# Routed attention and a gated long convolution in one kernel: first head pair routed by head, scores per head for four pairs, some exponential sums on GpSimd, a new order of the work

## The chip, the cores and the metric

The kernel runs on one core of one Trainium2 chip. The metric is the device time of one execution in microseconds (us). Its engines are TensorE (PE; its weight loads are listed as PEld), VectorE (DVE), ScalarE (ACT), GpSimd (POOL) and the DMA queue of SyncE (SP). DMAs are issued from SP, POOL and ACT. Everything is written by hand: which engine does an operation and in which order stands in a table in the program.

## The reference

```python
# attention: q, k, v are 4 batches x 8 heads x 768 x 64; centroids 8 heads x 16 x 64
q_assign = argmax(q_n . c_n);  k_assign = argmax(k_n . c_n)     # nearest of 16 centroids
mask = q_assign[..., :, None] == k_assign[..., None, :]
scores = where(mask, q k^T / 8, -1e9)
attn = exp(scores - max);  attn = attn / (sum(attn) + 1e-9);  attn_out = attn v
# long convolution, x = attn_out as 4 x 768 x 512
x1, x2, x3 = split(x @ w_proj, 3)
y = x1 * irfft(rfft(x2) * rfft(filter)) * x3
out = y @ w_out                                                 # 4 x 768 x 512, float32
```

## The kernel before

**The unit of work is a pair of heads**: 16 pairs (4 batches of 4). `prepare(n)` makes the operands of pair n: the raw rows of q and k come in by DMA and are turned so that the 64 features lie on partitions (DVE transposes, L134; for pair 0 alone PE transposes, L125, which ACT copies out of PSUM). `routing(n)` multiplies with the normalised centroids (`SIM`, psR<-qT,cbd), and DVE finds the nearest one in four steps: transpose R1 (L158), maximum R2 (L162), compare R3 (L166), transpose back R7 (L171). A product with a constant (`TB`, psR<-ohT,tb) turns the one-hot rows into mask rows. Together with -q and k (casts `C`, L141 to L145) they make the tile `aug`, so that one product gives score and mask penalty at once. For pair 0 the mask rows go straight from PSUM into `aug` (`W`, ACT L190 or DVE L192, eight pieces); for the others by ACT or DVE into `ohS` (`R8`) and by four DMAs into `aug`.

**Then six key tiles sk per pair**: `scores` (PE, psB or psBS<-aug), the exponential (`E`, ACT), `values` (`PV`, psO<-P,v: 128 keys against 768 query columns of two heads) and `sums` (`A`, DVE L271, 128x1536 float32: acc += P, five in a row per pair, each needing the one before). Four `P` tiles rotate: one comes free when its `PV` and its `A` have run. Pairs 0 to 3 use psB: three banks of 512 columns, so a tile's two heads of 768 come as three pieces with an `E` each (L256). From pair 4 on there is one psBS tile of three banks and one `E` of 1536 columns (L233). `finish` multiplies acc with ones (`D`, psR<-acc,ones) for the denominators; in pairs 0 and 1 the last key tile is not added by DVE but multiplied with ones by PE (`DS`, psR<-P,ones, table `PES`). The reciprocals go through DMAs, and DVE makes xT (`X`).

**After each four pairs a batch is convolved**: sums and differences of halves (`XB`), the projection (`U`), the spectrum (`F`), products with the filter's spectrum (`M`, DVE L368; `Y`, DVE or POOL L375, L381), the inverse (`I`), gates (`G`, `GE`, `GM`), their product (`Y2`, DVE or POOL L436) and the output product (`O`), copied to `ob` (three tiles in rotation) and written by a DMA of SP (L458). The batch's work lies between the score and value products of the next four pairs; after the last pair only convolution is left.

**The order** is one compressed table, `ORDER`: it names every operation of the program in turn with its engine. Each engine runs its own operations in that order, and tiles are handed out and come free in it too. An operation of POOL that is listed in `PORT` (two SBUF inputs or a cast) also waits for the last such operation of DVE before it in the table. `NWU` products of zeros (`WU`, psR<-ob) fill PE's waits at the start: 36 operations of two products each. PSUM has eight banks: at first three for small things (`R`), two for `O` and three for `B`.

Of the kernel before, what the change touches and what calls it, by code (L numbers as in the profile page):

```python
# [28 lines left out]
FRONT = 1  # L29
NWU = 36  # L30
NF = 4
PES = [1, 1] + [0] * 14
DIRECT = 1
# [12 lines left out]
PCLASSES = dict(S=(1, [128, 2 * S], F32), B=(3, [128, 512], F32), O=(1, [128, 2, 512], F32), R=(8, [128, 512], F32))  # L46
# [11 lines left out]
def adder(nc, eng):  # L58
    return {"DVE": nc.vector.tensor_tensor, "POOL": nc.gpsimd.tensor_tensor}[eng]

# [16 lines left out]
def program(io):  # L77
# [15 lines left out]
    def load_front(n, j):  # L93
        b, r = divmod(n, 4)
        for hp in range(2):
            def f(hp=hp):
                nc.sync.dma_start(P["raw", n, j][:].rearrange("p (t e d) -> p t e d", t=NT, e=2)[:, :, hp],
                                  (q, k)[j][b, 2 * r + hp].rearrange("(p t) d -> p t d", t=NT))
            op(("LF", n, j, hp), "SP", f, [], [(("raw", n, j), hp)])
# [19 lines left out]
    def front_turn(n, j):  # L119
        where = lambda ch: ("BR"[j], "t", n, j, ch)  # L120
        half = lambda ch: P[where(ch)][:, :HS]
        for ch in range(2):
            def f(ch=ch):
                for t in range(3):
                    nc.tensor.transpose(half(ch)[:, ts(t, 128)], P["raw", n, j][:, ts(3 * ch + t, 128)], C["ident"])  # L125
            op(("FT", n, j, ch), "PE", f, [("raw", n, j), "ident"], [where(ch)])
        for ch in range(2):
            def f(eng, ch=ch):
                copier(nc, eng)(P["qT", n, j][:, ts(ch, HS)], half(ch))
            op(("FE", n, j, ch), ("ACT", "DVE"), f, [where(ch)], [(("qT", n, j), ch)])  # L130
# [6 lines left out]
    def cast(n, j, hp):  # L137
        def f(eng):
            o, i = P["aug", n][64 * hp:64 * hp + 64, hp, j], P["qT", n, j][64 * hp:64 * hp + 64]
# [6 lines left out]
        op(("C", n, j, hp), ("ACT", "DVE", "POOL") if j else ("ACT", "DVE"), f, [("qT", n, j)], [(("aug", n), ("x", j, hp))])  # L146

    def routing(n):
# [6 lines left out]
        op(("SIM", n), "PE", f, [("qT", n, 0), ("qT", n, 1), "cbd"], [("R", "sim", n)])  # L155

        def f():
            nc.vector.transpose(P["sT", n][:], P["R", "sim", n][:, :HS])  # L158
        op(("R1", n), "DVE", f, [("R", "sim", n)], [("sT", n)])

        def f():
            nc.vector.tensor_reduce(P["mx", n], P["sT", n][:].rearrange("p (n c) -> p n c", c=NC), axis=AX, op=Alu.max)  # L162
        op(("R2", n), "DVE", f, [("sT", n)], [("mx", n)])

        def f():
            nc.vector.tensor_tensor(P["cand", n], P["sT", n][:].rearrange("p (n c) -> p n c", c=NC),  # L166
                                    P["mx", n][:].unsqueeze(2).to_broadcast([128, 24, NC]), op=Alu.is_equal)
        op(("R3", n), "DVE", f, [("sT", n), ("mx", n)], [("cand", n)])

        def f():  # L170
            nc.vector.transpose(P["ohT", n][:], P["cand", n][:].rearrange("p n c -> p (n c)"))  # L171
        op(("R7", n), "DVE", f, [("cand", n)], [("ohT", n)])
# [5 lines left out]

        if n < DIRECT:
            for j in range(2):  # L180
                for hp in range(2):
                    for ch in range(2):
                        def f(eng, j=j, hp=hp, ch=ch):
                            z = 2 * ch + j
                            r = 32 * (2 - hp)
                            rows = slice(32 * z, 32 * z + 32)
                            o, i = P["aug", n][r:r + 32, hp, j, ts(ch, HS)], P["R", "tb", n][rows, :HS]
                            m = C["mk"][rows, hp if j else 2:hp + 1 if j else 3]
                            if eng == "ACT":
                                nc.scalar.activation(o, i, Act.Relu, **(dict(scale=m) if j else dict(bias=m)))  # L190
                            else:
                                nc.vector.tensor_scalar(o, i, m, 0.0, op0=Alu.mult if j else Alu.add, op1=Alu.max)  # L192
                        op(("W", n, j, hp, ch), ("DVE", "ACT"), f, [("R", "tb", n), "mk"], [(("aug", n), ("o", j, hp, ch))])
            return
# [22 lines left out]
    def scores(n, sk):  # L217
# [19 lines left out]
        for b, some in enumerate((parts[:1], parts[1:3], parts[3:])):  # L237
            def f(b=b, some=some):
                products(some, lambda h, c, w: P["B", n, sk, b][64 * h:64 * h + 64, ds(c - 512 * b, w)])
            need = []  # L240
            for hp, lo, hi in some:
                need += [(("aug", n), ("x", j, hp)) for j in range(2)]
                halves = {(1, sk // 3)} | {(0, x // HS) for x in (lo, hi - 1)}
                need += [(("aug", n), ("o", j, hp, ch) if n < DIRECT else ("o", j, hp)) for j, ch in sorted(halves)]
# [487 lines left out]
def routed_attention_and_long_convolution(ctx: ExitStack, tc: tile.TileContext, q, k, v, c, wp, ff, wo, out):  # L732
# [14 lines left out]
    C = {}  # L747
# [58 lines left out]
    for name in ("RO", "R", "RS"):  # L806
        banks[name].close()
# [73 lines left out]
```

## Time and profile before

| | |
|---|---|
| time, 3 runs | 366.17 us median (365.65 to 366.39) |
| the profiled execution | 365.99 us, its span 364.3 us |
| PE busy | 355.0 us, 97% |
| DVE busy | 333.6 us, 92% |
| ACT busy | 254.8 us, 70% |
| POOL busy | 90.5 us, 25% |
| first score product, first value product | at 16.13 us, at 21.77 us |
| last product ends, last write is issued | at 360.02 us, at 361.14 us |

How to read it: span times count from the first instruction, and the execution's own time is 1.7 us longer than its span. In a row of groups stand line, engine, operation, tiles (out<-in), shape and count, then busy time in us and mean ns of one, then idle time of the engine ahead of it. In a row of the timeline stand start, length, engine and what; "x20" are merged instructions. All products but transposes have line 84, so they are told apart by their tiles. A logical float32 product shows as two records.

### The profile page before, as it was taken

To read this page: it belongs to the slowest core of one execution; us is meant where nothing else is said; L and a number is where in the kernel's file an instruction comes from. 1 tells how busy PE (TensorE), PEld (TensorE's weight loads), DVE (VectorE), ACT (ScalarE), POOL (GpSimd) and SP (SyncE) were. 2 spreads that over 40 slices of the span, in tenths; PEclk is the share of its full clock that TensorE was granted. 3 is DMA by queue.
4 is the path that set the end of the run, shared out by engine and by line. 5 is a ranking of instruction groups with operands and counts; after the bars stand their busy time and mean duration, and the time that the engine had idled before them with its cause. 6 is when DMAs were issued, how large, how long until landed. Compare 5 with 4: busy or idle time off the path is not lost.

```text
span 364.3 us, 8367 instructions
## 1 busy us (share of the span) xinstructions
PE 355.0 (97%) x3273; PEld 191.2 (52%) x3273; DVE 333.6 (92%) x458; ACT 254.8 (70%) x353; POOL 90.5 (25%) x126
## 2 busy tenths in 40 slices
PE   8899999999999999999999999999999999999995
PEld 3344445454355565545445656554445555555673
DVE  7899999999989999999888999998998999975992
ACT  6899888897786877786755768778776667214332
POOL 5333300023245314230112430211000211160651
PEclk9999999999999999999999999999999999999999
DMA  8676966588794455536344236255202310112204
GB/s 164 109 128 130 226 146 124 106 151 129 144 137 90 110 111 107 118 87 168 80 82 114 56 55 134 51 139 144 75 13 68 120 45 2 46 47 88 87 2 173
DMA packets 116167, 37.37 MB, mean 103 GB/s; under 512 B 104353, under 2 KB 109793, under 8 KB 116129
## 3 DMA queue, kind: packets, MB, share of 16 engines
q1 hardware_dynamic: 112688, 31.31, 39.7%
q0 software_dynamic: 3296, 5.51, 7.3%
q8 instruction: 25, 0.41, 0.5%
q14 instruction: 14, 0.11, 0.1%
q10 hardware_dynamic: 144, 0.03, 0.0%
HBM read 30.97 MB, written 6.39 MB: 103 GB/s over the span
## 4 chain that ended last, share of the span: by engine, by line
PE 71%; DVE 18%; issue 4%; ACT 3%; DMA 2%; SPq 1%; POOL 0%; DVEq 0%; ACTq 0%
PE psO L84 27%; PE psR L84 25%; PE psBS L84 10%; DVE acc L271 8%; PE psSR L84 4%; DVE tm L368 4%; PE psB L84 3%; ACT P L233 2%; PE psOR L84 1%; DVE qT L134 1%; DVE y L381 1%; DMA raw<-in_q_dram 1%; DMA aug<-ohS 1%; SPq L109 1%; DMA out_dram<-ob 0%
## 5 line engine op out<-in xcount | busy, mean ns | idle before, releaser
L84 PE MATMUL psO<-P,v 128*64 128x512 f32 (+1 forms) x768 | 139.4, 487 | 0.2 <-ACT P L233 0.2
L233 ACT ACTIVATE P<-psBS 128x1536 f32<-128x1536 f32 x72 | 104.6, 1452 | 42.2 <-PE psBS L84 36.8
L271 DVE TENSOR_TENSOR acc<-acc,P 128x1536 f32<-128x1536 f32 x62 | 108.4, 1749 | 3.1 <-ACT P L233 1.0
L84 PEld LDWEIGHTS psO<-P,v 128*64 128x64 f32 x768 | 54.5, 136 | 66.9 <-issue 56.3
L84 PEld LDWEIGHTS <-aug 96*64 96x64 bf16 (+1 forms) x768 | 44.9, 110 | 33.4 <-issue 12.5
L84 PE MATMUL psBS<-aug 96*64 96x512 bf16 (+3 forms) x576 | 59.9, 327 | 0.3 <-ACT P L233 0.2
L256 ACT ACTIVATE P<-psB 128x512 f32<-128x512 f32 x72 | 38.1, 598 | 4.8 <-PE psB L84 4.6
L84 PE MATMUL psR<-xT,wpj 128*64 128x384 bf16 x416 | 40.8, 326 | 0.1
L84 PEld LDWEIGHTS <-wpj 128*64 128x64 bf16 x512 | 30.3, 110 | 13.5 <-issue 1.8
L375 POOL TENSOR_TENSOR y<-tm,tm 128x512 bf16<-128x512 f32 x13 | 16.4, 1273 | 63.5 <-DVE tm L368 52.2
L84 PEld LDWEIGHTS <-y 128*64 128x64 bf16 x440 | 24.9, 110 | 13.1 <-DVE y L436 0.6
L134 DVE STREAM_TRANSPOSE qT<-raw 128x768 f32<-128x768 f32 x30 | 28.8, 964 | 0.2
L436 POOL TENSOR_TENSOR y<-yy,g 128x768 bf16<-128x768 f32 (+1 forms) x14 | 20.5, 1474 | 32.2 <-DVE g L403 13.1
L330 POOL TENSOR_TENSOR xb<-xT 128x384 bf16<-128x384 bf16 x12 | 11.2, 931 | 68.0 <-DVE acc L271 27.1
L271 DVE TENSOR_TENSOR acc<-P,P 128x1536 f32<-128x1536 f32 x16 | 27.8, 1737 | 0.1
L141 POOL CAST aug<-qT 64x768 bf16<-64x768 f32 x13 | 10.7, 819 | 68.9 <-DVE acc L271 56.0
L368 DVE TENSOR_TENSOR tm<-psR,hm 128x512 f32<-128x512 f32 x40 | 25.2, 681 | 1.7 <-PE psR L84 1.3
L84 PE MATMUL psB<-aug 128*64 128x256 bf16 (+3 forms) x192 | 22.3, 328 | 0.9 <-DVE aug L192 0.6
L143 ACT ACTIVATE aug<-qT 64x768 bf16<-64x768 f32 x25 | 21.0, 841 | 1.6 <-PE psBS L84 1.1
L84 PE MATMUL psR<-uv,fw 128*64 128x512 bf16 x156 | 20.2, 379 | 0.1
L398 ACT COPY g<-psR 128x384 f32<-128x384 f32 x25 | 11.5, 483 | 12.0 <-PE psR L84 11.8
L84 PE MATMUL psR<-wpj,xb 128*64 128x512 bf16 x160 | 19.2, 379 | 0.0
(160 smaller groups left out, 439.0 us busy)
## 6 DMA issues: line engine op xcount, KB each, us to landing
rb<-dr SPq DMA_DIRECT2D x32, 192.0 KB, 3.4
out_dram<-ob SPq DMA_DIRECT2D x23, 256.0 KB, 2.2
raw<-in_q_dram SPq DMA_DIRECT2D x60, 96.0 KB, 3.1
raw<-in_k_dram SPq DMA_DIRECT2D x60, 96.0 KB, 3.4
v<-in_v_dram POOLq DMA_DIRECT2D x8, 384.0 KB, 4.2
v<-in_v_dram SPq DMA_DIRECT2D x8, 384.0 KB, 4.3
wpj<-in_moe_w_proj_dram POOLq DMA_DIRECT2D x12, 128.0 KB, 3.8
aug<-ohS SPq DMA_DIRECT2D x60, 24.0 KB, 2.7
```

The costliest lines, as they stand in the source:

```text
L84: pe = lambda out, l, r, st, sp: nc.tensor.matmul(out, l, r, start=st, stop=sp)
L134: nc.vector.transpose(P["qT", n, j][:], P["raw", n, j][:])
L141: copier(nc, eng)(o, i)
L143: nc.scalar.mul(o, i, -1.0)
L233: nc.scalar.activation(P["P", n, sk][:, :, :S], P["S", n, sk][:].rearrange("p (e s) -> p e s", e=2), Act.Exp, scale=-0.125)
L256: nc.scalar.activation(o, i, Act.Exp, scale=-0.125)
L271: nc.vector.tensor_tensor(P["acc", n], a[:, :, :S], P["P", n, sk][:, :, :S], op=Alu.add)
L330: adder(nc, eng)(P["xb", n][:, e], x[:, :, 0], x[:, :, 1], op=(Alu.add, Alu.subtract)[e])
L368: nc.vector.tensor_tensor(P["tm", b, i, r, cs], P["R", "f", b, i, cs], hm[i][:, s], op=Alu.mult)
L375: adder(nc, eng)(P["y", b, i][:, r], P["tm", b, i, r, 0], P["tm", b, i, r, 1], op=alu)
L398: copier(nc, eng)(P["g", b, dt][:, ts(ch, HS)], P["R", "g", b, dt, ch, 2][:, :HS])
L436: adder(nc, eng)(P["y2", b, dt][:, a:z], P["yy", b, dt][:, a:z], P["g", b, dt][:, a:z], op=Alu.mult)
```

## The change

1. Pair 0 is prepared head by head. A tile now holds q and k of one head, the first q is loaded through ACT's queue and the other three through SP's; `SIM` makes two rounds of half the width, R1, R2, R3, R7 run twice on 192 columns, `TB` is eight narrow products per head with a shifted window of a constant, and the scores of head 0 need only head 0. DVE copies one head's transposes out of PSUM, ACT the other's.
2. Pairs 0 to 3 have two psB tiles of two banks: one head of a key tile (768 columns) each, with one `E` of 768 columns. `R` has two banks instead of three until pair 4.
3. `A` may run on POOL, and does 17 times of 80. `DS` is gone (`PES` is zero): five `A` in every pair.
4. 20 `WU` instead of 36.
5. The last two output tiles are written in halves, and outputs of the last batch may be written by ACT's queue.
6. Parts of the tables' preparation may go to POOL or ACT, and the whole order is new.

```diff
-NWU = 36
+NWU = 20
-PES = [1, 1] + [0] * 14
+PES = [0] * 16
-PCLASSES = dict(S=(1, [128, 2 * S], F32), B=(3, [128, 512], F32), O=(1, [128, 2, 512], F32), R=(8, [128, 512], F32))
+PCLASSES = dict(S=(1, [128, 2 * S], F32), B=(2, [128, 1024], F32), O=(1, [128, 2, 512], F32), R=(8, [128, 512], F32))
...
+    def load_first(hp):
+        for j in range(2):
+            def f(j=j):
+                dma = nc.sync if hp or j else nc.scalar
+                dma.dma_start(P["raw", 0, hp][:].rearrange("p (t j d) -> p t j d", t=NT, j=2)[:, :, j],
+                              (q, k)[j][0, hp].rearrange("(p t) d -> p t d", t=NT))
...
+    def first_routing(hp):
+        W = HS // 2
+        def f():
+            for z in range(4):
+                pe(P["R", "sim", 0, hp][32 * z:32 * z + 32, :W], C["cb0"][:, hp], P["qT", 0, hp][:, ts(z, W)], True, True)
+        nearest((0, hp), W, f, [("qT", 0, hp), "cb0"])
+        def f():
+            for c in range(2):
+                for ch in range(2):
+                    for j in range(2):
+                        g = 64 * ch + 32 * j
+                        a = 16 + 32 * (2 * ch + c) + 16 * (j - hp)
+                        pe(P["R", "tb", 0, hp][g:g + 32, ts(c, W)], C["tbx"][:, a:a + 32], P["ohT", 0, hp][:, :W], True, True)
...
+        for hp in range(2):
+            def f(hp=hp):
+                products(((hp, 0, 512), (hp, 512, S)), lambda h, c, w: P["B", n, sk, hp][64 * h:64 * h + 64, ds(c - S * hp, w)])
...
+            def f(hp=hp):
+                nc.scalar.activation(P["P", n, sk][:, hp, :S], P["B", n, sk, hp][:, :S], Act.Exp, scale=-0.125)
...
     def sums(n, sk):
-        def f():
+        def f(eng):
             a = P["P", n, 0] if sk == 1 else P["acc", n]
-            nc.vector.tensor_tensor(P["acc", n], a[:, :, :S], P["P", n, sk][:, :, :S], op=Alu.add)
-        op(("A", n, sk), "DVE", f, [("P", n, sk), ("P", n, 0) if sk == 1 else ("acc", n)], [("acc", n)])
+            adder(nc, eng)(P["acc", n], a[:, :, :S], P["P", n, sk][:, :, :S], op=Alu.add)
+        op(("A", n, sk), ("DVE", "POOL"), f, [("P", n, sk), ("P", n, 0) if sk == 1 else ("acc", n)], [("acc", n)])
...
+        op(("OD",) + key, ("SP", "ACT") if b == B - 1 else ("SP",), f, [("ob",) + key], [])
...
-                    if b == B - 1 and t == NT - 1:
+                    if b == B - 1 and t >= NT - 2:
                         for c in range(2):
                             output(b, t, w, c * DM // 2, (c + 1) * DM // 2)
...
-    "c-jTQ17H?v7zWVi)tBq%a&4<++qP}nwr$(CZQHhOo40!oKoA%hp@{DZM^a=$9wbK+WJ6&TLo!506oeo)Vjvpwp)Ts72^ymiBG44gPzSZq0F4j_aZ"
+    "c-jrpgI`^J901@ie>Jr3J?Gpz)@rp?tJ$lzYPN0Lwr$(CZQHhOdwbu1;rToO2xXx>l!H)+gshMavO^w74-7dW3n&njfppLnGC?;8aAk%LF2zKU7?"
```

What the new table makes of DVE's work at the first routing. Before, from the first transpose of the similarities on (g and identb belong to the convolution's tables, inv too; qT<-raw is pair 1's):

```order
L158 STREAM_TRANSPOSE sT_77<-psR_136 128x384
L532 SCALAR_TENSOR_TENSOR g_118<-g_118 128x384
L162 TENSOR_REDUCE mx_78<-sT_77 128x24
L532 SCALAR_TENSOR_TENSOR g_116<-g_116 128x384
L166 TENSOR_TENSOR cand_80<-sT_77,mx_78 128x384
L479 CAST identb<-ident 128x128
L171 STREAM_TRANSPOSE ohT_82<-cand_80 128x384
L134 STREAM_TRANSPOSE qT_65<-raw_62 128x768
L192 TENSOR_SCALAR aug_66<-psR_136,mk 32x384
L663 COPY inv<-psR_134 128x384
L192 TENSOR_SCALAR aug_66<-psR_136,mk 32x384 x2
L675 COPY inv<-psR_135 128x384
```

And after, from the same place on:

```order
L156 STREAM_TRANSPOSE sT_77<-psR_134 128x192
L160 TENSOR_REDUCE mx_78<-sT_77 128x12
L165 TENSOR_TENSOR cand_80<-sT_77,mx_78 128x192
L156 STREAM_TRANSPOSE sT_77<-psR_135 128x192
L170 STREAM_TRANSPOSE ohT_82<-cand_80 128x192
L160 TENSOR_REDUCE mx_79<-sT_77 128x12
L148 TENSOR_SCALAR aug_66<-qT_64 64x768
L165 TENSOR_TENSOR cand_81<-sT_77,mx_79 128x192
L202 TENSOR_SCALAR aug_66<-psR_135 32x384
L170 STREAM_TRANSPOSE ohT_82<-cand_81 128x192
L200 TENSOR_SCALAR aug_66<-psR_135,mk 32x384
L136 STREAM_TRANSPOSE qT_65<-raw_62 128x768
```

The table work has left this place; the two heads' steps are interleaved at half width, and a cast of -q (L148) stands between them. Behind these rows DVE has the other four mask pieces, with pair 1's second transpose between them.

POOL in the middle of the program, before (the end of batch 0's products Y2, then XB and batch 1's Y):

```order
L436 TENSOR_TENSOR y_125<-yy_122,g_116 128x768
L330 TENSOR_TENSOR xb_99<-xT_97 128x384
L115 DMA v_71<-in_v_dram 128x2x384
L330 TENSOR_TENSOR xb_101<-xT_98 128x384
L330 TENSOR_TENSOR xb_99<-xT_97 128x384
L375 TENSOR_TENSOR y_114<-tm_109,tm_110 128x512
L375 TENSOR_TENSOR y_114<-tm_106,tm_107 128x512
```

And after, the same stretch (acc<-P are sums A of pairs 8 and 9):

```order
L451 TENSOR_TENSOR y_125<-yy_122,g_117 128x768
L345 TENSOR_TENSOR xb_99<-xT_97 128x384
L286 TENSOR_TENSOR acc_76<-acc_76,P_72 128x1536
L345 TENSOR_TENSOR xb_100<-xT_96 128x384
L345 TENSOR_TENSOR xb_99<-xT_97 128x384
L286 TENSOR_TENSOR acc_76<-P_72,P_75 128x1536
L286 TENSOR_TENSOR acc_76<-acc_76,P_73 128x1536
L286 TENSOR_TENSOR acc_76<-acc_76,P_72 128x1536
L390 TENSOR_TENSOR y_114<-tm_110,tm_108 128x512
L390 TENSOR_TENSOR y_114<-tm_109,tm_106 128x512
L286 TENSOR_TENSOR acc_76<-acc_76,P_75 128x1536
```

Four of pair 9's five sums stand on POOL, the first three behind one another; pairs 5, 6 and 10 have two there, seven other pairs one and five none.

ACT at the program's end, before (its outputs are written by SP):

```order
L454 COPY ob_130<-psSR_3475 128x512
L454 COPY ob_128<-psSR_3473 128x512
L454 COPY ob_129<-psR_134 128x512
L454 COPY ob_128<-psOR_3684 128x512
L454 COPY ob_129<-psOR_3685 128x512
```

And after:

```order
L469 COPY ob_129<-psOR_3652 128x512
L473 DMA out_dram<-ob_129 128x512
L469 COPY ob_130<-psSR_3432 128x512
L469 COPY ob_128<-psSR_3431 128x512
L473 DMA out_dram<-ob_128 128x512
L473 DMA out_dram<-ob_129 128x256
L469 COPY ob_130<-psSR_3430 128x512
L473 DMA out_dram<-ob_130 128x512
L469 COPY ob_130<-psSR_3432 128x256
L473 DMA out_dram<-ob_130 128x256
```

ACT now issues five of the eight last writes itself, and its last copy goes into the tile, ob_130, that the write just ahead of it still reads. DVE copies the other three halves, and SP writes two of them.

More of the change, by code (lines that the diff above doesn't have):

```diff
@@ L154, in f @@
                        True, True)
-        op(("SIM", n), "PE", f, [("qT", n, 0), ("qT", n, 1), "cbd"], [("R", "sim", n)])
-        def f():
[L158 to L172, printed above, removed]
+        nearest((n,), HS, f, [("qT", n, 0), ("qT", n, 1), "cbd"])
         def f():
@@ L693, in program @@
         for j in range(2):
[L694 removed]
+            load_blocks(n, j)
         load_v(n)
```

279 lines of the change are left out of this document (152 added, 127 removed).

## The prediction, made before the result was known

> **What bounds the kernel now.** I read the page's busy times first, then the sums by stretch, to see whether the busiest engine is busy throughout.
>
> ```profile
> PE 355.0 (97%) x3273; PEld 191.2 (52%) x3273; DVE 333.6 (92%) x458; ACT 254.8 (70%) x353; POOL 90.5 (25%) x126
> PEclk9999999999999999999999999999999999999999
> 0.00:21.77 21.77, 18.43 (x151) 8.54 (x153) 17.93 (x47) 16.95 (x29) 10.92 (x45) 1.00 0.73 137
> 21.77:360.02 338.25, 336.54 (x3124) 182.68 (x3120) 315.26 (x411) 237.23 (x324) 79.55 (x82) 1.00 0.46 100
> L84 PE MATMUL psR<-ob 128*64 128x512 bf16 x72 | 11.4, 453 | 2.1 <-DVE ob L590 1.5 <-DVE inv L663 0.6
> ```
>
> From the first value product (21.77) to the last product (360.02) PE is busy 336.54 of 338.25 us at a full clock: it waits 1.7 us in all. DVE is close behind. The first two rows are the page's, the next two sums by stretch. So the time has three parts: the front up to 21.77, the amount of PE's work, and the end from 360.02. In the front 18.43 us are busy, but 11.4 of them are the products of zeros (psR<-ob), so PE's true work there is about 7 us. That front is where time can be had. The timeline says what it waits for:
>
> ```profile
> 1.53 4.47 PE L84 MATMUL psR<-ob 128*64 128x512 bf16 x20 [1.53 <-DVE ob L590]
> 5.93 0.87 PE L125 MATMUL psR<-ident,raw 128*128 128x128 f32 x6
> 6.69 0.25 DVE L564 TENSOR_SCALAR c<-c,cs 128x64 f32<-128x64 f32 x1
> 8.96 0.85 PE L84 MATMUL psR<-qT,cbd 128*32 128x384 f32 x8
> 9.74 3.21 PE L84 MATMUL psR<-ob 128*64 128x512 bf16 x28
> 14.84 1.15 ACT L190 ACTIVATE aug<-psR,mk 32x384 bf16<-32x384 f32 x2 [0.68 <-DVE aug L192]
> 16.01 1.28 ACT L256 ACT_TABLE_LOAD   x1
> 16.13 0.62 PE L84 MATMUL psB<-aug 96*64 96x512 bf16 x4 [0.27 <-ACT aug L190]
> 17.30 2.06 ACT L256 ACTIVATE P<-psB 128x512 f32<-128x512 f32 x4
> 21.77 1.46 PE L84 MATMUL psO<-P,v 128*64 128x512 f32 x8
> 33.10 0.85 PE L84 MATMUL psR<-acc,ones 128*32 128x384 f32 x8
> 35.20 1.48 PE L84 MATMUL psO<-P,v 128*64 128x512 f32 x8
> ```
>
> A chain on DVE and ACT: similarities at 8.96, mask pieces until 15.99, the table of the exponential, the first exponential at 17.30. The row at 33.10 is pair 0's denominator product, that at 35.20 its last value product.
>
> **The front, by head.** These rows price DVE's steps; ACT's row at 14.84 gives 0.57 for one mask piece there.
>
> ```profile
> L158 DVE STREAM_TRANSPOSE sT<-psR 128x384 f32<-128x384 f32 x16 | 9.2, 572 | 1.6 <-PE psR L84 1.5
> L171 DVE STREAM_TRANSPOSE ohT<-cand 128x384 bf16<-128x384 bf16 x16 | 9.2, 572 | 1.2 <-PE psR L84 0.9
> L166 DVE TENSOR_TENSOR cand<-sT,mx 128x384 bf16<-128x384 f32 x16 | 8.8, 551 | 0.3
> L162 DVE TENSOR_REDUCE mx<-sT 128x24 f32<-128x384 f32 x16 | 8.8, 547 | 0.3
> L134 DVE STREAM_TRANSPOSE qT<-raw 128x768 f32<-128x768 f32 x30 | 28.8, 964 | 0.2
> L145 DVE TENSOR_SCALAR aug<-qT 64x768 bf16<-64x768 f32 x7 | 3.8, 550 | 0.1
> L192 DVE TENSOR_SCALAR aug<-psR,mk 32x384 bf16<-32x384 f32 x5 | 3.1, 616 | 1.2 <-ACT aug L190 1.1
> L398 DVE COPY g<-psR 128x384 f32<-128x384 f32 x4 | 2.2, 547 | 0.0
> L271 DVE TENSOR_TENSOR acc<-acc,P 128x1536 f32<-128x1536 f32 x62 | 108.4, 1749 | 3.1 <-ACT P L233 1.0
> ```
>
> Ten fill operations (the 20 products of 1.53) still stand ahead of the first transposes, so these start at 5.93 as before. DVE ends the centroids' scaling at 6.94; with identb's cast (0.22) moved ahead of it, 7.16. Two copies out of PSUM like L398's (1.09) and four small centroid copies, of which two (0.44) are needed: 8.7. Head 0's similarities take half of 0.85: 9.1. The half-width steps are not in the trace. The two transposes, 572 ns for 384 columns and 964 for 768, make 1.02 ns a column and 0.18 fixed, so 0.37 for 192; bounds are half (0.28) and all (0.57), and I take 0.37 for all four. Up to head 0's first mask piece DVE has seven of them and a cast: 9.1 + 7 x 0.37 + 0.55 = 12.2. The pieces take turns on the two engines, as the release at 14.84 shows: DVE's ends at 12.9, ACT's two at 14.0, and the table's 1.28 gives the first exponential at 15.3, **2.0 us sooner**. Head 1 follows on DVE: a mask piece (0.62), pair 1's transpose (0.96), three pieces (1.85), a transpose, a piece: 19.0. PE holds one more score product, and the first value product comes at about 19.4, 2.4 sooner.
>
> But not all of this lasts. PE's next fixed point is the denominator product at 33.10, and DVE must bring it five sums now, not four: from 19.0 a cast (0.55), pair 1's four routing steps (2.24), five sums (8.7) and two transposes (1.9), with some 0.2 of waiting, make 32.6. That is 0.5 sooner; the last value product behind it loses two queued pieces and comes some 1.5 sooner. **I take -1.5, bounds -0.5 and -2.4.** The 16 fill operations removed (32 products, some 5 us by the x72 row) lie in these waits: nothing, unless the clock falls (a rival). `TB`'s and `SIM`'s extra narrow products lie there too. The filter tables' work moved to POOL and ACT must be ready before 11; POOL was busy for only 10.92 of the first 21.77 us, so I count nothing.
>
> **Sums by PE gone, exponentials re-cut.**
>
> ```profile
> L84 PE MATMUL psR<-P,ones 128*32 128x384 f32 x16 | 1.7, 492 | 0.0
> L256 ACT ACTIVATE P<-psB 128x512 f32<-128x512 f32 x72 | 38.1, 598 | 4.8 <-PE psB L84 4.6
> L233 ACT ACTIVATE P<-psBS 128x1536 f32<-128x1536 f32 x72 | 104.6, 1452 | 42.2 <-PE psBS L84 36.8
> ```
>
> The 16 `DS` products leave a saturated PE: 1.7 us. The first eight stood just ahead of DVE's 33.10, and may only lengthen a wait. **-1.5, bounds -0.8 and -1.7.** The exponentials: 854 ns for 1024 more columns is 0.834 a column, so 768 take 811; less the overlap of 69 ns that 38.1 for 72 shows, 48 x 0.742 = 35.6 against 38.1 us of ACT. Six copies of the inverse's table instead of two, some 0.4 each, give 1.6 of it back. ACT is off the path after 40 us: nothing.
>
> **Seventeen sums on POOL.**
>
> ```profile
> L375 POOL TENSOR_TENSOR y<-tm,tm 128x512 bf16<-128x512 f32 x13 | 16.4, 1273 | 63.5 <-DVE tm L368 52.2 <-DVE xT L318 9.7 <-DVE y L375 1.5
> L436 POOL TENSOR_TENSOR y<-yy,g 128x768 bf16<-128x768 f32 x8 | 14.6, 1828 | 28.3 <-DVE g L403 13.1 <-DVE dn L305 10.6 <-DVE xT L318 3.6
> L271 DVE TENSOR_TENSOR acc<-acc,P x62: 1682/1753/2012, 25.5 to 310.8; 128x1536 f32<-128x1536 f32 x62
> 312.66 0.85 PE psSR L84 x8
> ```
>
> POOL: 555 ns for 256 more columns, 2.17 a column; 1536 columns make 1.83 + 768 x 2.17 ns = 3.49 us, twice DVE's 1.75. Bounds are 2.7 (the upper 768 columns at DVE's 1.14 ns) and 5.2 (half as much again, if the sum meets DVE at a shared resource, as the 2012 of an overlapped sum hints). DVE loses 15 of its 78 sums (26 us) and takes on Y, GE, R8 and others, some 9: about 17 net, 5% of it. The Trainium skill speaks against such a move: GPSIMD Engine Reference, section Engine selection, would leave two-input elementwise work to VectorE, as GpSimd is about twice slower at it; by that rule this part is no gain, 0 at best, and the total 363.5. The row of stretches decides what relief is worth: PE has only 1.7 us of visible waiting, part of it behind DVE. **-0.5, bounds -2.0 and 0**, when the longer sums stay hidden. Their cover: pairs follow each other by (312.66 - 33.10) / 15 = 18.6 us, and pair 9's five sums in a row take 4 x 3.49 + 1.75 = 15.7. Behind a sum on POOL queue its Y, Y2 and casts, and behind its end the `P` tile, its next exponential and PE.
>
> **The end.**
>
> ```profile
> 358.99 1.03 PE L84 MATMUL psOR<-wout,y 128*64 128x512 bf16 x8
> 360.11 0.58 ACT L454 COPY ob<-psOR 128x512 f32<-128x512 f32 x1 [0.71 <-PE psOR L84]
> 360.34 0.42 DVE L454 COPY ob<-psSR 128x256 f32<-128x256 f32 x1 [1.97 <-DMA out_dram<-ob]
> out_dram<-ob SPq DMA_DIRECT2D x23, 256.0 KB, 2.2
> ```
>
> Call the last product's end T, before 360.02. The last write left at 361.14, T + 1.1. Now three halves come last, 0.43 each at PE's pace, so the last full tile is done at T - 1.3, copied by ACT at T - 0.7, written by T + 1.5, and only then may the last half be copied into the same ob_130: its write leaves at about T + 1.9, 0.8 later. T itself may come 0.3 sooner, as the product that feeds these outputs moves from POOL (1.0) to DVE (0.6). **+0.5, bounds -0.3 and +1.0.**
>
> Sum against the profiled execution's 365.99: -1.5 - 1.5 - 0.5 + 0.5 = -3.0, so **363.0 us**; that execution stood 0.2 below the median of 366.17. The bounds add up to 359.6 and 366.2.
>
> **The rivals.**
>
> *POOL's sums bind (slower).* For it: acc is one tile and a pair's sums are a chain; POOL was let wait for DVE's sums, and no sum on POOL is in the trace. Against: pair 9 has 2.9 us to spare. It decides from 4.2 us a sum on. At 5.2 pair 9 takes 22.6, 4.0 over its 18.6; where POOL has the last sum (pairs 6, 9 and 10), the denominator product waits 3.4 longer, of which I let a half reach PE in pairs 6 and 10; with relief gone: 363.0 + 0.5 + 4.0 + 3.4 = 371; where only pair 9 binds, 367.5. I price it at 368. The Trainium skill, SBUF — State Buffer, section Who interferes with whom, makes it likelier: a VectorE instruction with two SBUF inputs and a GpSimd one lock each other out for the whole instruction; the stretched 2012 agrees.
>
> *The lead is lost behind DVE (no change).* The early DVE is full up to pair 3, and only one sum there moves. Lead 0, `DS` worth 0.8, the end +0.5: 365.7.
>
> *The clock falls in the thinner front.* The rows of 1.53 and 9.74 show 20 products in 4.47 us against 28 in 3.21: half pace at first. With the fill gone, if half pace returns near 15 for another 4.4 us, 2.2 are lost: 365.2. Against: the reckoning above leaves PE no single wait of over 2 us. The Trainium skill, TensorE: Matmul & The Clock Gate, section HAM oscillation, asks for idle gaps above some 3.4 us; by it nothing happens here.
>
> *More is won.* The lead stays whole (-2.4), `DS` 1.7, relief 1.5, the end +0.1: 360.5.
>
> **How the numbers follow.** My forecast (361.2 to 364.6) has 0.55, POOL's sums 0.14, the lost lead 0.10, the clock 0.07, more 0.14. About 0.2% (0.7 us) is what a measurement here tells from no change. Faster: 0.55 + 0.14 + 0.07 = 0.76; same 0.10; slower 0.14. The range reaches from 360.2, most of the better case, to 366.3, the bounds' worst, and leaves POOL's case out.
>
> **What would show it.** In the changed profile: the first exponential near 15.3 and first value product near 19.4; pair 0's denominator product at 32 to 33; sums on POOL of 3.5 us, and PE waiting nowhere for more than some 0.5 us behind one; the last write about 2 us behind the last product. Wrong would be a value product after 21, sums of 4.5 us and more, waits of PE named after acc or P in pairs 6, 9 or 10, or a half-paced row after 10.

## The result, and the profile after

The changed kernel takes 369.25 us (median of 14 runs, 366.34 to 370.97); the kernel before, beside it, 366.22 (14 runs, 365.60 to 367.69). The measured ratio is 1.0065, with a 95% interval of 1.004 to 1.009: slower by 0.65%, where 363.0 and faster were forecast. (The two medians alone lie 3.0 us, 0.83%, apart; with runs that scatter so, a difference of two medians is uncertain by about 1 us, as the interval's 0.25% to either side shows.) The runs also scatter over 4.6 us, those of before over 2.1. The profiled execution took 369.67 us (span 367.96), 3.68 more than that of before.

The page's busy times and its row of the granted clock, in 40 slices:

```profile
PE 350.7 (95%) x3255; PEld 191.5 (52%) x3255; DVE 322.8 (88%) x459; ACT 248.6 (68%) x321; POOL 150.6 (41%) x145
PEclk9899999999999999999999999999999999999999
```

PE works 4.3 us less than before and still ends later: it waits more, and in the second slice its clock is lower. PE's waits, dearest first (in total, times, longest); one of 1.5 us at the very start, for the zeros of the fill, is the same before and after:

```profile
PE psR L127 <- DMA raw<-in_q_dram: 2.9, 1, 2.9
PE psB L86 <- ACT P L271: 1.8, 3, 1.3
PE psO L86 <- DMA v<-in_v_dram: 1.6, 1, 1.6
PE psR L86 <- DVE ohT L170: 1.5, 2, 1.1
PE psB L86 <- ACT aug L198: 1.2, 1, 1.2
PE psBS L86 <- ACT P L256: 0.8, 1, 0.8
```

Before, PE's list had no wait for a transfer at all. Of the other kinds it had these, much shorter:

```profile
PE psR L84 <- DVE ohT L171: 0.3, 2, 0.2
PE psB L84 <- ACT aug L190: 0.3, 1, 0.3
PE psBS L84 <- ACT P L233: 0.2, 1, 0.2
```

The timeline of the front (start, us, engine, line; in brackets the idle time ahead and who ended it):

```profile
2.26 0.90 POOL L117 DMA_DIRECT2D v<-in_v_dram  x1
8.86 1.19 PE L127 MATMUL psR<-ident,raw 128*128 128x128 f32 x6 [2.90 <-DMA raw<-in_q_dram]
9.85 1.48 PE L127 MATMUL psB<-ident,raw 128*128 128x128 f32 x6
12.73 1.01 PE L86 MATMUL psR<-qT,cb 128*32 128x192 f32 x16
16.23 0.55 DVE L202 TENSOR_SCALAR aug<-psR 32x384 bf16<-32x384 f32 x1
16.81 0.57 ACT L198 ACTIVATE aug<-psR,mk 32x384 bf16<-32x384 f32 x1 [1.93 <-DVE aug L202]
17.49 0.63 DVE L200 TENSOR_SCALAR aug<-psR,mk 32x384 bf16<-32x384 f32 x1 [0.30 <-ACT aug L198]
18.15 0.57 ACT L198 ACTIVATE aug<-psR,mk 32x384 bf16<-32x384 f32 x1 [0.77 <-DVE aug L200]
18.74 1.28 ACT L271 ACT_TABLE_LOAD   x1
20.03 2.23 ACT L271 ACTIVATE P<-psB 128x768 f32<-128x768 f32 x3
24.16 1.46 PE L86 MATMUL psO<-P,v 128*64 128x512 f32 x8
```

The first transposes come at 8.86, not 5.93, behind a load. The second six take 1.48 us, where six took 0.87 before: half the pace. The sums by stretch (PE's busy time is the first number after the length, the granted clock stands ahead of the DMA share) show it; the stretches are those at whose borders the trace's clock record changes or could change:

```profile
5.80:9.21 3.41, 0.51 (x5) 0.38 (x4) 1.72 (x7) 0.81 (x2) 3.33 (x3) 1.00 1.07 217
9.21:12.63 3.42, 3.42 (x16) 2.11 (x14) 1.44 (x4) 2.99 (x6) 1.62 (x9) 0.50 0.32 51
12.63:16.04 3.41, 2.27 (x34) 0.99 (x34) 3.02 (x11) 2.20 (x5) 0.00 (x0) 1.00 0.78 156
```

While PE waits, the 16 DMA engines are full (1.07); then PE is busy all of 3.42 us at half clock. First exponential 20.03 (17.30 before), first value product 24.16 (21.77): the front costs 2.39 us. From there to the last product, and later on the way:

```profile
24.16:363.23 339.07, 334.97 (x3138) 184.03 (x3134) 304.55 (x412) 231.88 (x295) 135.38 (x95) 1.00 0.46 100
56.44 1.08 PE L86 MATMUL psO<-P,v 128*64 128x512 f32 x4 [1.64 <-DMA v<-in_v_dram]
78.32 0.23 DVE L320 RECIPROCAL dn<-dn 128x12 f32<-128x12 f32 x1 [1.58 <-DMA dn<-den]
82.92 0.84 PE L86 MATMUL psBS<-aug 96*64 96x512 bf16 x8 [0.79 <-ACT P L256]
362.62 0.60 PE L86 MATMUL psSR<-wout,y 128*64 128x256 bf16 x8
365.15 0.34 ACTq L473 DMA_DIRECT2D out_dram<-ob  x1
```

339.07 us, against 338.25 before: +0.82, with two new waits of PE in it, 1.64 for pair 2's values and 0.79 behind a late load of denominators. The last product ends at 363.23, the last write leaves 1.92 later, and the span ends 4.73 behind that product (4.26 before). The sum: 2.39 + 0.82 + 0.47 = 3.68.

When the loads arrive is in the trace's packet records: the end of the last packet of each of the first raw loads (768 packets of 256 bytes each, counted off in order of time on each queue), and of pair 0's value load:

```
                     SP 1st  SP 2nd  SP 3rd  SP 4th  ACT    v
before               3.42    4.23    5.01    6.21    -      9.5
changed              3.55    4.99    7.46    -       4.42   7.2
```

Head 1 is transposed first and needs SP's second and third. PE started 1.40 us behind the packet that ended at 7.46. (The expectations below have 6.99 for this 7.46 and 5.8 for the 6.21 of before.)

### The profile page after: what moved, and what is told of

Read it like the earlier page. It is cut to its first block, busy times and chain, and to the rows that moved or that the text cites. A ratio compares the mean times of both kernels' runs of the same rounds, so it can differ in the third digit from the quotient of the medians.

```text
span 368.0 us, 8311 instructions
## 1 busy us (share of the span) xinstructions
PE 350.7 (95%) x3255; PEld 191.5 (52%) x3255; DVE 322.8 (88%) x459; ACT 248.6 (68%) x321; POOL 150.6 (41%) x145
## 4 chain that ended last, share of the span: by engine, by line
PE 71%; DVE 10%; DMA 7%; SPq 3%; issue 3%; ACT 2%; POOL 1%; ACTq 0%; DVEq 0%
PE psO L86 25%; PE psR L86 18%; PE psBS L86 11%; PE psBR L86 10%; DVE acc L286 4%; PE psSR L86 4%; DMA raw<-in_q_dram 2%; DMA v<-in_v_dram 2%; PE psOR L86 2%; PE psB L86 1%; SPq L111 1%; DMA rb<-dr 1%; DMA raw<-in_k_dram 1%; SPq L233 1%; POOL y L390 1%
## 5 line engine op out<-in xcount | busy, mean ns | idle before, releaser
L286 DVE TENSOR_TENSOR acc<-acc,P 128x1536 f32<-128x1536 f32 x50 | 87.3, 1745 | 5.8 <-POOL acc L286 2.5
L286 POOL TENSOR_TENSOR acc<-acc,P 128x1536 f32<-128x1536 f32 x14 | 48.4, 3455 | 58.9 <-DVE cand L165 18.3
L271 ACT ACTIVATE P<-psB 128x768 f32<-128x768 f32 x48 | 36.7, 810 | 6.2 <-PE psB L86 3.2
L86 PE MATMUL psR<-xT,wpj 128*64 128x384 bf16 x248 | 25.3, 326 | 0.0
L390 POOL TENSOR_TENSOR y<-tm,tm 128x512 bf16<-128x512 f32 x11 | 13.9, 1277 | 25.2 <-DVE tm L383 14.5
L86 PE MATMUL psB<-aug 96*64 96x512 bf16 (+1 forms) x192 | 20.9, 328 | 2.9 <-ACT P L271 1.8
L286 DVE TENSOR_TENSOR acc<-P,P 128x1536 f32<-128x1536 f32 x13 | 22.7, 1748 | 0.3 <-ACT P L271 0.2
L383 DVE TENSOR_TENSOR tm<-psR,hm 128x512 f32<-128x512 f32 x26 | 16.8, 682 | 2.0 <-PE psR L86 1.1
L333 DVE SCALAR_TENSOR_TENSOR xT<-osb,rb 128x768 bf16<-128x768 f32 x16 | 16.2, 1011 | 1.2 <-DMA rb<-dr 1.2
L86 PEld LDWEIGHTS <-xb 128*64 128x64 bf16 x192 | 11.1, 110 | 8.9 <-issue 0.3
```

What stands on the lines that cost most here:

```text
L86: pe = lambda out, l, r, st, sp: nc.tensor.matmul(out, l, r, start=st, stop=sp)
L271: nc.scalar.activation(P["P", n, sk][:, hp, :S], P["B", n, sk, hp][:, :S], Act.Exp, scale=-0.125)
L286: adder(nc, eng)(P["acc", n], a[:, :, :S], P["P", n, sk][:, :, :S], op=Alu.add)
L333: nc.vector.scalar_tensor_tensor(P["xT", n], P["osb", n][:, :S], P["osb", n][:, S:S + 1], P["rb", n], op0=Alu.add, op1=Alu.mult)
L383: nc.vector.tensor_tensor(P["tm", b, i, r, cs], P["R", "f", b, i, cs], hm[i][:, s], op=Alu.mult)
L390: adder(nc, eng)(P["y", b, i][:, r], P["tm", b, i, r, 0], P["tm", b, i, r, 1], op=alu)
```

## The experiments

Theory F: the loss is made in the front, by a load that PE waits for and that shares the DMA engines with the early value load. C: the clock's fall is a loss of its own. V: so are the later waits for value loads. Q: the third load is late by its own place in the queue, whatever the value load does. L: the loss is made later, by GpSimd's sums or the end. Diffs show rows of the engines' instruction lists. Times are medians; each ratio is against the kernel before on the same chip, with its 95% interval.

**Value load later.** On POOL:

```diff
-L117 DMA v_69<-in_v_dram 128x2x384
 L660 MEMSET w 128x4
...
 L554 TENSOR_TENSOR g_118<-g_118,yy_121 128x384
+L117 DMA v_69<-in_v_dram 128x2x384
 L506 MEMSET tbx 128x160
```

> Edit: the changed kernel with pair 0's value load issued by GpSimd behind the third filter table's analysis (near 8.5 us) instead of at 2.26. Theory F (the loss is made in the front: PE's first transposes wait 2.9 us for the third load of SP's queue, which shares the 16 DMA engines with the early value load, and the granted clock then halves for 3.4 us): the third raw load's last packet comes near 5.8 instead of 6.99, the transposes start at 7.0 to 7.6 instead of 8.86, the clock probably stays whole, and the time is 366 to 367.5 against the changed kernel's 369.3. Rival Q (the load's place in the queue is the cause, the value load is innocent): the transposes still start after 8.5 and the time is 368.7 to 369.5. Rival L (the loss is made later, by GpSimd's sums or the end): the front moves and the time does not, 368.7 to 369.5.

366.11 us (0.9988, 0.9971 to 1.0005), 3.1 less than the changed kernel. The third load's last packet ended at 5.87:

```profile
7.09 0.85 PE L127 MATMUL psR<-ident,raw 128*128 128x128 f32 x6 [1.65 <-DMA raw<-in_q_dram]
17.06 2.23 ACT L271 ACTIVATE P<-psB 128x768 f32<-128x768 f32 x3
14.98:18.40 3.42, 1.32 (x14) 0.77 (x13) 3.30 (x6) 3.20 (x4) 3.05 (x7) 1.00 0.43 69
18.40:21.81 3.41, 3.41 (x23) 0.98 (x19) 1.70 (x3) 3.05 (x6) 1.85 (x3) 0.50 0.67 134
22.56 1.46 PE L86 MATMUL psO<-P,v 128*64 128x512 f32 x8
```

F holds: one DMA issue, moved, takes the whole loss away. Q and L fall as its cause. The other runs bear it out: in the six traces of the changed program with the early value load the third load's last packet ended at 7.2 to 8.0, in the eight with the later one at 5.9 to 6.4. But the clock fell all the same, later, behind a stretch with 1.32 us of work, and the time is only that of before.

**Head 0 first.** On PE, with both heads' transposes into psB:

```diff
-L127 MATMUL psR_134<-ident,raw_61 128x128 x3
-L127 MATMUL psR_135<-ident,raw_61 128x128 x3
 L127 MATMUL psB_143<-ident,raw_60 128x128 x3
...
-L86 MATMUL psR_134<-qT_64,cb_149 32x192 x4
-L86 MATMUL psR_135<-qT_63,cb_149 32x192 x4
+L86 MATMUL psR_134<-qT_63,cb_149 32x192 x4
+L127 MATMUL psB_143<-ident,raw_61 128x128 x3
+L127 MATMUL psB_144<-ident,raw_61 128x128 x3
+L86 MATMUL psR_135<-qT_64,cb_149 32x192 x4
```

> Edit: the changed kernel with head 0's six transposes first on PE, and head 1's (with their copies) behind head 0's similarities; loads as they were. Head 0's two loads are the first of SP's queue and the one on ACT's, whose last packets came at 3.5 and 4.4. Theory F: transposes at 6.0 to 6.5, head 0's similarities near 9, a full clock or a short fall, the first exponential at 16 to 17.5 instead of 20.0, and 365.5 to 367 us. Rival Q predicts the same here. Rival L: the first exponential comes 2.5 sooner or more and the time is still over 368.

366.18 us (0.9993, 0.998 to 1.0007), with the early value load left in. Transposes at 5.92, first exponential at 17.61. F again: what is transposed first must be what lands first. The clock was at half from 16.24 for two stretches, and the first value product came at 23.62.

**More fill.** Seven fill operations ahead of the first transposes, on PE two such products each:

```diff
-NWU = 20
+NWU = 27
...
 L86 MATMUL psR_135<-ob_128 64x512
+L86 LDWEIGHTS ob_128
+L86 MATMUL psR_134<-ob_128 64x512
...
```

> Edit: the changed kernel with seven more fill operations (14 products of zeros, about 3.1 us) ahead of the first transposes, so that PE is busy while it waits for the load. The transposes cannot come sooner than 8.9. If the halved clock costs what its 3.4 us show (half of it, 1.7 us, in theory F one part of the loss): clock 1.00, the first exponential near 18.5 instead of 20.0, and 367.3 to 368.2 us. If the clock costs nothing, since DVE sets the pace there: 369 to 369.8.

367.03 us (1.0022, 1.0002 to 1.0043), 2.2 less than the changed kernel, though the transposes came at 8.60. Clock 1.00 from 7.25 on, first exponential at 18.48, first value product at 22.61, last product at 358.66: 336.05 us for the body in this trace, with no wait for v. C holds: 2.2 between the medians, 1.6 by the ratios, for 1.7 expected. The scatter (365.1 to 369.0) stays, and it goes with the clock: the three executions at a mean clock of 0.998 and more took 365.1 to 365.4, the nine below it 366.0 to 369.0.

**Both: value load later, head 0 first** (the first two diffs).

> Edit: the value load later (as in the run that moves it alone) and head 0's transposes first. Theory F, and the rest of the change worth what was reckoned: transposes at 6.0 with no wait, head 1's ready before they are wanted, the first exponential at 15.3 to 16.5 and 363 to 365.5 us. Rival L: over 367. If 365.5 to 367, the front held most of the loss but the sums and the end win nothing.

366.37 us (1.0007, 0.9992 to 1.0022). The expectation failed. Transposes at 5.41, but the similarities waited 0.54 for the centroids on DVE and came at 8.95, the first exponential at 17.60, and the clock fell at 18.33. Where the loads are in time, two other things set the front.

**Later load and fill in every wait.** 22 fill operations more:

```diff
-NWU = 20
+NWU = 42
```

> Edit: the changed kernel, pair 0's value load later, and 22 fill operations more (42 in all): 4 ahead of the first transposes, 5 and 2 ahead of the two heads' mask products, 6 and 5 ahead of the first and third score products, where PE waited in the run with the later value load. Theory C (the clock is set anew every 3.41 us; a stretch in which PE streams for a third of the time or less is followed by one at half pace, and the phase of these stretches differs from run to run, which scatters the times): no halved stretch, first exponential at 17 to 17.5, first value product near 21.2, then the 336 us to the last product that the run with more fill showed, about 364 us and runs that lie within 1 us of each other. Rival (the first value product hangs on DVE and ACT alone; the clock costs nothing): 366.1 as without the fill, scatter as before.

366.32 us (1.0009, 0.9995 to 1.0022): failed, with a clock of 1.00. The fill itself waited: it writes the two banks of psR, and they were still read. The first exponential moved from 17.06 to 18.15. The time is the rival's, but it decides nothing on C, since the edit brought a wait of its own.

**Pair 2's value load by GpSimd.** On POOL (and the same row out of SP's list):

```diff
 L622 MEMSET aug_68 32x768
+L117 DMA v_71<-in_v_dram 128x2x384
 L144 CAST aug_68<-qT_64 64x768 x2
```

> Edit: the changed kernel with nothing but pair 2's value load given from SP's queue (issued at 49.2, PE waited 1.8 us for it at 56.4) to GpSimd's, behind pair 2's zeros (near 33). If that wait is a loss of its own (theory V): no wait of PE for v, 1.7 us sooner, 367.0 to 367.9; some 366.6 if the 0.8 wait at 83 goes with it. If what PE gains there is lost again at the next wait: over 368.8.

369.39 us (1.0074, 1.0052 to 1.0095): the median did not move. The traced execution had no wait for v and took 367.26, but most did not. V alone does not explain the usual run.

**The kernel before with less fill.** The 14 fill operations between pair 0's similarities and its mask product, and two behind:

```diff
-NWU = 36
+NWU = 20
```

> Edit: the kernel before with 16 of its 36 fill operations left out (14 of the 16 between the similarities and the mask product of pair 0, two behind), nothing else. Theory C: PE streams for less than a third of 9.3 to 12.7, the stretch behind it goes at half pace, the times scatter, and the median is 366.8 to 368.2 instead of 366.2. Rival (products of zeros do nothing for the time): 366.2, clock 1.00.

367.15 us (1.0026, 1.0016 to 1.0036): about 1 us dearer. C holds in the old kernel too:

```profile
8.96:12.38 3.42, 0.64 (x8) 0.11 (x1) 3.38 (x9) 3.41 (x7) 0.30 (x3) 1.00 0.87 137
12.38:15.79 3.41, 2.44 (x17) 1.12 (x16) 2.31 (x4) 1.93 (x4) 3.07 (x7) 0.50 0.38 60
15.79:19.20 3.41, 3.29 (x18) 1.47 (x16) 3.10 (x5) 3.13 (x5) 0.00 (x0) 0.50 0.83 130
```

**Later load, fill, pair 2's load by GpSimd** (three of the diffs above).

> Edit: all three together: value load of pair 0 later, 22 fill operations more, pair 2's value load by GpSimd. Theories C and V, and the rest of the change worth what was reckoned (2.0 for the body, the end 0.5 to 0.8 dearer): 363 to 364.5 us and a clock of 1.00. If the body wins nothing: 365.5 to 366.5.

366.85 us (1.0018, 1.0006 to 1.003): failed like the run with 42 fill operations, by the same banks (first exponential 18.19), and with a new wait of 0.5 for a transfer at 112.74.

**All of it, fill into psO, a fourth output tile.**

```diff
-pe(P["R", "w", i][64 * h:64 * h + 64], wz[:, :64], wz[:, :512], True, True)
+pe(P["O", "w", i][64 * h:64 * h + 64, 0], wz[:, :64], wz[:, :512], True, True)
...
-ob=(3, [128, DM], F32)
+ob=(4, [128, DM], F32)
```

> Edit: pair 0's value load later; pair 2's by GpSimd; 22 fill operations more, all fill into the bank of psO, which is free until the first value product, so that no fill waits for a bank as it did in the run with 42; a fourth output tile, so that the last half does not wait for a write. Theories C, V and S (S: the times scatter because SP's queue, which issues one transfer after the other from 19 to 56 us, runs late by what its long issues and the front cost): clock 1.00, first exponential near 17.1, first value product near 21.2, the last write 1.1 behind the last product: 362.5 to 364 us. Rival (the body's win of 2 us seen in single traces is lost in most runs): 365.5 and more.

366.26 us (0.9999, 0.9989 to 1.0009): failed, with the front as expected (17.16, 21.29, clock 1.00). What it won was spent on two waits of PE:

```profile
39.34 0.41 PE L86 MATMUL psO<-ob 128*64 128x512 bf16 x2 [1.17 <-ACT osb L304]
116.89 1.30 PE L86 MATMUL psO<-P,v 128*64 128x512 f32 x6 [0.95 <-DMA v<-in_v_dram]
```

The first is a fault of the edit: an old fill operation that stands behind pair 0's value products now wanted their bank. The second is a load that stood late in SP's order and had been in time for a later PE.

**GpSimd's sums back on DVE** (value load later). On DVE, 17 such rows:

```diff
 L286 TENSOR_TENSOR acc_76<-acc_76,P_72 128x1536
+L286 TENSOR_TENSOR acc_76<-acc_76,P_75 128x1536
 L160 TENSOR_REDUCE mx_79<-sT_77 128x24
```

> Edit: the changed kernel with pair 0's value load later and all 17 sums of GpSimd given back to DVE, in the same places of the order. GpSimd's sums took 3.46 us each, DVE's some 1.76, so DVE gets some 30 us more work in a body in which it was busy for 93%. Theory R (the relief is real, some 0.5 us or more): slower than 366.1, 367 to 371. Rival P (GpSimd's sums bind somewhere): faster than 366.1.

386.94 us (1.0567, 1.0552 to 1.0582), 20.8 more than with the sums on GpSimd, and far more than expected: the new order leaves DVE no room for them. L and P fall.

**The kernel before with the early value load.** On its POOL:

```diff
 masks.py:199 AFFINE_SELECT ident<-ident 128x128
+L115 DMA v_69<-in_v_dram 128x2x384
...
-L115 DMA v_69<-in_v_dram 128x2x384
```

> Edit: the kernel before with nothing but pair 0's value load issued at 2.2 instead of 5.8. Its first transposes need only the first two loads of SP's queue, whose packets ended at 4.2, and the second pair of transposes the next two (5.8). Theory F (the early value load hurts where a load that PE waits for is still under way): the first transposes hardly move (5.9 to 6.3), the next, at 7.4 before, come 1 to 1.7 later, 36 fill operations keep the clock: 366.2 to 367.5. If the early load by itself makes the whole 3 us: 368.5 and more.

368.39 us (1.0065, 1.0048 to 1.0081): by the ratio, this one issue costs the old kernel as much as the whole change did, and more than F's 367.5. A part is the clock's: three executions at a mean clock of 0.999 and more took 367.6 to 367.9, three at 0.995 took 368.9 to 369.5. The traced one is of the first kind. Its loads' last packets ended at 3.32, 4.77, 6.41, 8.20, and the second half of its transposes started 0.83 behind the last, after a wait of 2.02:

```profile
9.03 0.52 PE L125 MATMUL psB<-ident,raw 128*128 128x128 f32 x3 [2.02 <-DMA raw<-in_q_dram]
```

Its first value product moved by 1.60 (23.37) and its last product by 1.59 (361.61): what the front loses is lost at the end.

**Later load, pair 2's load by GpSimd, fourth output tile; fill as in the changed kernel.**

> Edit: pair 0's value load later, pair 2's by GpSimd and a fourth output tile, with the fill as in the changed kernel (20 operations). The run with the later load alone was 366.1. Theory V: the 0.5 to 0.7 us wait for v at 54 goes; the fourth tile brings the last write from 1.9 to some 1.1 behind the last product: 364.6 to 365.4, and the difference to the run with all of it is what the clock costs here, 1 to 2 us. Rival: 366.1, since SP is late anyway.

365.06 us (0.9981, 0.9958 to 1.0005), runs from 364.0 to 368.5. No wait for v. The traced execution, 366.85, had three stretches at half clock, and its first value product came 6.4 us behind the first exponential, where a full clock shows 4.1.

**The faults mended.** As in the run with all of it, but only the 22 new operations write psO, and pair 6's value load stands earlier in SP's list (by 15 places, not 30):

```diff
-pe(P["R", "w", i][64 * h:64 * h + 64], wz[:, :64], wz[:, :512], True, True)
+pe((P["R", "w", i] if i < 20 else P["O", "w", i][:, 0])[64 * h:64 * h + 64], wz[:, :64], wz[:, :512], True, True)
...
 L117 DMA v_71<-in_v_dram 128x2x384
+L117 DMA v_69<-in_v_dram 128x2x384
 L329 DMA rb_91<-dr_174 64x768 x2
```

> Edit: value loads of pair 0 later and of pair 2 by GpSimd, a fourth output tile, 22 fill operations more, of which all write the bank that is free until the first value product (the 20 old ones write where they did), and pair 6's value load some 30 places earlier in SP's order. Theories C and V: clock 1.00, first value product at 21.3, no wait of PE for v or for a bank in use, last write 1.1 behind the last product, 362.5 to 364 us, with less scatter than 364.0 to 368.5. Rival S (what is won ahead is taken again by transfers that come late): a new wait of PE for a transfer between 30 and 130 us, and 365 or more.

**364.42 us (0.9956, 0.994 to 0.9972)**, runs from 363.95 to 365.81: faster than both kernels.

```profile
7.16 0.85 PE L127 MATMUL psR<-ident,raw 128*128 128x128 f32 x6
16.47:19.88 3.41, 3.41 (x37) 1.72 (x35) 3.29 (x6) 3.40 (x6) 2.00 (x4) 1.00 0.76 140
21.18 1.02 PE L86 MATMUL psO<-P,v 128*64 128x512 f32 x4
21.18:357.51 336.33, 334.60 (x3138) 183.94 (x3134) 305.11 (x412) 231.96 (x295) 135.10 (x96) 1.00 0.46 100
358.99 0.42 DVE L469 COPY ob<-psR 128x256 f32<-128x256 f32 x1 [1.84 <-DMA out_dram<-ob]
```

What C, F and V said of it came true together: the clock stayed whole, PE waited for no value load, the front is 0.6 shorter than before and the body 1.9. The end failed: the last write left at 359.70, 2.2 behind the last product and not 1.1, since the last row's copy waited for a write that still read its tile. With the same four tiles the run of 365.06 had 0.6.

**The changed kernel traced again** (no edit).

> No edit: a second trace of the changed kernel, one execution. If every execution loses the same: first transposes at 8 to 9, one stretch or two at half clock by 23 us, PE's wait for v near 56 and that for P near 83. If the later waits come only where SP runs late: its waits differ, and its time goes with them.

368.40 us in one execution. The front repeats to 0.05 us (8.86, 20.00, 24.12, half clock from 9.27); the later waits do not. Pair 2's load was issued at 48.31 instead of 49.23 and nobody waited for it; the wait behind the denominators came again, at 81.90 (1.08). So the front was lost in the same way in both traces, while the later waits differ with what SP issues late.

**The best kernel with the value load early again** (the first diff, backwards).

> Edit: the kernel that measured 364.42 (later value load, fill into a free bank, fourth output tile, pair 2's and pair 6's value loads earlier) with pair 0's value load put back to 2.26 us, nothing else. Theory F: PE waits for the third raw load until 8.6 to 8.9 instead of 7.2 (four more fill operations cover a part), the clock falls or not by its phase, and what the front loses stays lost to the end: 366 to 367.5 us, that is 1.5 to 3 more. If the cost is only the clock's (fill keeps it): 364.5 to 365. If a late front is caught up behind DVE: 364.4.

365.91 us (0.9994, 0.9979 to 1.001), 1.5 more and just under the range of F. In the traced execution (367.0) the clock stayed at 1.00; transposes at 8.47, first value product 1.30 later than in the best kernel. Its last product comes 2.58 later, and the rest is covered by one later wait, of 1.64:

```profile
64.20 0.84 PE L86 MATMUL psB<-aug 128*64 128x512 bf16 x8 [1.64 <-DMA aug<-ohS]
```

## Why the prediction was wrong

The step that failed is this: "Ten fill operations (the 20 products of 1.53) still stand ahead of the first transposes, so these start at 5.93 as before." It looked at what PE has queued and not at what the transposes wait for. Two moves of DMA issues broke it, and neither was costed: the loads' order (head 1 needs SP's second and third, where the first transposes needed the first and second before) and pair 0's value load, which went from 5.82 to 2.26, so that its packets (5.19 to 7.23) ran in among those of the third load. Its early issue costs 1.5 us in the best kernel, 2.1 in the kernel before and 3.1 in the changed kernel, by the medians. The Trainium skill says as much (DMA: Bandwidth & Descriptors, section Issuing engines are not separate DMA queues): transfers that different engines start run on the same 16 DMA engines and interleave. The trace agrees: with the value load out of the way the third load's last packet ends at 5.87 instead of 7.46. The loads' order is as much a part of the loss: with head 0 first and the early value load left in, it was gone too (366.18).

The forecast put the first value product at 19.4; it came at 24.16. The 4.76 us are, by the rows above:

- **Start of the transposes:** 8.86 for 5.93, 2.93.
- **Transposes to similarities:** 3.87 for 3.17 (9.1 less 5.93), 0.70. This is the clock: in the run with more fill, at full clock, it was 2.58, so the fall cost 1.29 and the forecast's copies were 0.59 too long.
- **Similarities to first exponential:** 7.30 for 6.2, 1.10. The half-width steps were right (0.38, 0.35, 0.36 and 0.33 for 0.37). The mask pieces were mis-sized: I let ACT do its two in a row from 12.9 to 14.0, but all four take turns, DVE, ACT, DVE, ACT, from 16.23 to 18.72. At the forecast's start that alone makes 14.7 of 14.0; the first piece came 3.5 behind the similarities, not 3.1.
- **First exponential to first value product:** 4.13 for 4.1. Right.

**The clock** was a rival with a chance of 0.07. Its price, 2.2, was about right (the run with more fill won 2.2 between the medians, 1.6 by the ratios), its chance too small, and the reason given against it, no single wait of over 2 us, was twice wrong: there was one of 2.90, and none is needed. The Trainium skill's rule there (TensorE: Matmul & The Clock Gate, section HAM oscillation), idle gaps above some 3.4 us, let nothing happen here. The measurement decides against it: the clock fell behind gaps of 2.9 us, and in the run with the later value load behind waits of 1.3 at most.

**"But not all of this lasts"** found no support. In single traces, time lost or won in the front reaches the end nearly whole: 1.60 at the first value product and 1.59 at the last product in the kernel before, 1.43 and 1.15 from the run with more fill to the best one. No run had a front two microseconds ahead of before, so a lead of that size stays untested.

**`DS` and the relief**, -2.0, were right in sum and not in their shares: the body takes 336.05 and 336.33 us where no load is late, against 338.25, so 1.9 to 2.2 less. But PE's waits there stayed as they were (1.71 before, 1.67 and 1.73 in these two), so all of it is work that left PE and the 0.5 for the relief does not show as less waiting; that the sum came out is luck to that extent. (The sums must leave DVE all the same: given back, they cost 20.8.) In the changed kernel two waits took this back, and more. The first of them was a move not costed either: pair 2's value load went from POOL's queue (37.28) to SP's (49.23), behind some forty issues that SP makes one after the other from 19 us on.

**POOL's sums** did not bind: 3.46 us each for 3.49 (3.44 to 3.47 over all 17), and PE's only wait behind acc is the 0.5 that before had too. The lock-out that the rival named is there, on DVE's side:

```profile
171.45 3.46 POOL L286 TENSOR_TENSOR acc<-acc,P 128x1536 f32<-128x1536 f32 x1 [2.41 <-DVE acc L286]
173.22 2.10 DVE L165 TENSOR_TENSOR cand<-sT,mx 128x384 bf16<-128x384 f32 x1
```

DVE's compare, which reads two tiles of SBUF, takes 0.55 us elsewhere; here it began during POOL's sum and ended 0.41 behind it. One more compare (0.91, at 94.29) and a product (1.17, at 291.98, for some 0.69 elsewhere) began during a sum; no wait of PE came of the three. **The end** was right: the last write at 1.92 behind the last product (1.9), the span 0.47 longer for 0.5.

**The sum's upper bound** was added up wrongly: -0.5, -0.8, 0 and +1.0 on 365.99 make 365.7, not 366.2 (that has the front's part at 0). The measured time lies above both.

What stays open: how the usual 369.3 us of the changed kernel divide among the later waits. Two traces show two patterns, moving one load did not change the median, and the number of half-clock stretches does not go with the time (an execution at a mean clock of 0.995 took 369.85, one at 0.987 took 367.15).

## What to carry to other kernels

Ahead of each first use of loaded data, list what else is on the DMA engines at that time, whoever issued it, and see that data land in the order in which they are used; a transfer that is needed late does harm by being early. Fill on PE that seems idle may hold the clock: take it away only where the real work of each stretch keeps PE busy. And where one queue issues without a pause, a later start there can come out as waits far behind, in other places in each run.

## What the runs showed of the hardware

The granted clock changes only at the borders of stretches of 3.41 us, whose phase differs from run to run. In the first 40 us of all 17 traces, a stretch at full clock in which PE was busy for 1.65 us or less was followed by one at half clock all ten times; with 1.85 or more that never came, and of five with 1.77 to 1.84 one fell. A stretch at half clock was followed by another when PE was busy for 2.68 us or less (2.44 above), and by the full clock from 2.77 on. So evenly thin work loses the clock without any long gap, and one kernel can have one to three such stretches in one run or another (the changed kernel's mean clock was 0.995 to 0.985; one stretch makes 0.0046). What one cost differs: some 1.4 us in the kernel before with the early value load (367.6 to 367.9 without, 368.9 to 369.5 with one), about 1 us for two together in the kernel before with less fill.

A PE that waited for a load started 0.8 to 1.4 us behind the end of its last packet (8.20 and 9.03; 5.87 and 7.09; 7.46 and 8.86).

A DVE instruction with two inputs from SBUF that began during a GpSimd sum ended only behind that sum (a compare of 0.55 us took 2.10), while the sum kept its 3.44 to 3.47 us.
